# Attention and a two-layer block on one core: batch 2's products with v in float32, a first pair of quarter products interleaved, sums and a branch rearranged

## The chip, the cores and the metric

The kernel runs on one core of one Trainium2 chip. The metric is device time in microseconds of one execution, lower is better. Engines: PE = TensorE, DVE = VectorE, ACT = ScalarE, POOL = GpSimd, SP = SyncE, whose queue issues nearly all DMAs.

## The reference

Eight batches, twelve heads, 448 tokens, head size 64; then 768 to 2048 to 768 features. Inputs are float32.

```python
scores = q @ k.T / sqrt(64) - log(448)
attn = 1 / (1 + exp(-scores))
x = (attn @ v)                      # heads side by side: 3584 x 768
h = x @ w_in                        # 768 x 2048
g = h - tanh(h)
out = g @ w_out                     # 2048 x 768
```

## The kernel before

**Tiles.** Features lie on the partitions and the 448 tokens of a batch along the free axis. Two heads share 128 partitions, so a batch has six *head pairs*. `stream` counts them through batches 1 to 7 as g = 0 to 41 and takes two per turn. For a pair, `units` makes scores (`scores`, L532), ACT turns them into the weights a (`weigh`, L543, a sigmoid), and `av` (L563) multiplies them with v into a PSUM tile acc, which ACT copies to x (`evac_x`, L575 or L577).

**Precision.** A float32 operand is mostly split into two float16 parts, the rounded value and the remainder, and a product takes three float16 matmuls. The rounded part comes from ACT (`activation` with Copy and a scale), the remainder from DVE (`scalar_tensor_tensor`): for a, `split_a` (L549, L550); for x and weights, `split` (L335, L338); for w_in's sums, `parts` (L197, L199). In `stream` the class constant `AV32` says from which batch on products with v are split (`splits`): before it, a and v go to PE as float32, where one call becomes two instructions. With the split come norms of v (`norm_v`, L473 on vn), its split (`prep_v`, L518, L519) and a scale at `evac_x`. There, an x without a scale has its square taken by ACT (L592), one with a scale by POOL (L594) in four of six pairs; POOL adds the squares up (L603).

**Stages.** Batch 0 runs in `first`, whose steps follow a string, `ORDER`, one letter a step: among others, R and r convert and split weights, B is the next step of the attention stream, P two steps of the output product, Z and S splits of w_in. Batch 1 multiplies by w_in as it is (`moe1`), and meanwhile `combine` builds, for each of eight column pairs q of w_in, sums of its four quarters (L209 to L215) and their split parts. `combine` is a generator with three steps per q, driven by `made`: 14 inside `moe1`, ten at the positions `MADE` in batch 1's output product. `load` brings a q's weights in, in part after the parts before have left the same place. Batches 2 to 7 use those sums: `moe1_quarters` needs seven quarter products per column pair instead of eight (`product`, L1004, 9 matmuls of 224 columns each; the names S3, A11, S2, A22, A12, S1, S4 say which sum of w_in is taken). Results c11, c21 lie in a PSUM tile py, c12, c22 in px; ACT copies c11 to c12 (L1052) and keeps c21 and c12 (L1053, L1060), DVE adds (L1074, L1075), and the curve of g follows one or two turns later (`square`, `cube`, `curve`, `rest`, `store`).

**Output product.** `moe2` multiplies g by w_out (L1137) into po, two PSUM tiles under the tag "mm" which py also uses, and evacuates po to o (L1157 on ACT, L1159 on DVE). After each of its 96 steps `second` runs what is due by a table of positions on a scale of 56: `BLOCKS1` or `BLOCKS` (attention of the next batch), `MADE`, `TAIL` (the end of g), `FILL` and `NORMS` (loads), `PARTS` (the scale of x, then its split into quarters, by `quarter_scales`). All engines' orders, SP's too from batch 1 on, are the order in which the code issues. The end: a flag says whether a general kernel must run instead (`build_kernel`, L1518 and L1519).

```python
def second(self, b, blocks, alone, events):
    ...
    for k, _ in enumerate(self.moe2(b, self.gs)):
        now = (k + 1) * 7 / 12
        while events and events[0][0] <= now:
            events.pop(0)[1]()
```

Of the kernel before, what the change touches and what calls it, by code (L numbers as in the profile page):

```python
# [10 lines left out]
F32 = mybir.dt.float32  # L11
# [8 lines left out]
P = 128  # L20
# [15 lines left out]

class Builder:

    AV32 = 2

    EARLY = 4
    LAND = ("o", "o", 2, "v", "v", "v", 1, 0, 3, 4, 5)
# [1 line left out]
        "lurmlorumsrrsrrmmlussmvvrrssvvrlrssvvrrvruvlssrurssvvrrssvlrrsvvvursrsvs"  # L44
        "vrrssvrsrrvvvvRrRrRRRMrRRRnRrRRGMRRwtMttRtRBtwRRtMwBgttMtRtRttMBttRtRttM"
        "tMBBtRttRMtBttMttDMtRxtRtBRAtDMtttADMtBttDMttAttAttMMtAtPPtaRRBPtBbtCaBC"
        "BACPtFCCPBPCPPBZPPCSBCPPBZCBCPPCCBPCCCSZBPCCCPCXBaaAPaPPPBAPaaaBBSPPSPSZ"
        "PSZSPPPPPPSPBPPZPPPNPZPSPZSSNNPPSZPZSSPPPP"
    )

    BLOCKS = (8, 11, 16, 20, 20, 20, 27, 32, 36, 36, 36, 43, 47, 51, 52)
    TAIL = (1, 2, 3, 4, 5)
    MADE = (5, 10, 12.5, 15, 21.5, 23, 25, 29.5, 31, 34)
    FILL = (44.5, 48.5, 53.5)
    END = (0.1, 1.7, 3)
    NORMS = (4.5, 10, 13, 24, 28)
    PARTS = (1.5, 5, 8.5, 10.5)
    ALONE = 11
    BLOCKS1 = (4, 7, 8, 11, 13, 16, 20, 20, 20, 27, 32, 36, 36, 36, 43, 47, 51, 52)

# [117 lines left out]
    def combine(self):  # L178

        h = self.NC // 2  # L180
        V = self.nc.vector
        at = self.NC * self.NB * 2 * 256
        tail = self.flat[:, at : at + 4 * self.NC * P].bitcast(F32).rearrange("p (t c n) -> p t c n", t=2, c=self.NC)
        loaded = {}

        def load(q):
            if q in self.AWAY:
                loaded[q] = [self.tp.tile([P, self.NC, P], F32, name="w32", tag="t", bufs=self.TP) for _ in range(2)]
                for i, t in enumerate(loaded[q]):
# [5 lines left out]
        def parts(q, o, src, between=lambda: None):  # L195
            t = self.tp.tile([P, self.NC, 2, P], F16, name="wt", tag="t", bufs=self.TP)
            self.nc.scalar.activation(t[:, :, 0], src, AF.Copy, scale=self.Swi)  # L197
            between()
            V.scalar_tensor_tensor(t[:, :, 1], src, self.Swi, t[:, :, 0], op0=ALU.mult, op1=ALU.subtract)  # L199
            self.nc.sync.dma_start(self.w1[q, :, o : o + 2], t.rearrange("p (o c) i n -> p o c i n", c=h))  # L200

        load(0)
        for q in range(self.NF // 2):
            top, bottom = loaded.pop(q)
            a11, a12, a21, a22 = top[:, :h], top[:, h:], bottom[:, :h], bottom[:, h:]
            ahead = (q in self.AWAY) != (q + 1 in self.AWAY)
            if ahead:
                load(q + 1)
            V.tensor_tensor(a22, a21, a22, op=ALU.add)  # L209
            V.tensor_tensor(a21, a11, a21, op=ALU.subtract)  # L210
            yield 1

            def sums():
                V.tensor_tensor(a11, a22, a11, op=ALU.subtract)
                V.tensor_tensor(a12, a12, a11, op=ALU.subtract)  # L215

            parts(q, self.S3, bottom, sums)
            yield 1
            parts(q, self.S2, top)
            if not ahead:  # L220
                load(q + 1)
            yield 1
# [383 lines left out]
    def stream(self):  # L606
# [34 lines left out]

        def parts_k(g):
            if g < G:
                K[g] = self.parts(qk[g][0], sc[g][0][:, 0:1], "K", not splits(g) and g not in (2, 3))

        def parts_q(g):
            if g < G:
# [74 lines left out]
        def keep(g, cs, aa):  # L722
            if splits(g):
                aa = [self.split_a(a) for a in aa]
                if len(self.xs) < NP and g >= self.NP * (self.AV32 - 1) + 2:
                    self.x_sums()
            todo.extend((g, c, a) for c, a in zip(cs, aa))

        for g in range(0, G, 2):
# [162 lines left out]
    def quarter_scales(self, xs):  # L892

        h = self.NC // 2
        m = self.token_norms(self.ps.tile([P, 2, 512], F32, name="nm", tag="sc", bufs=2)[:, 0])
        Sx, ix = self.x_scale(m)
        self.x_sums()
        xt = self.xt
        out = self.xparts()

        def parts(c, x, ops):
            self.split(out[:, ops, c, 0], out[:, ops, c, 1], x, Sx, True)

        def pair(x):
            return x.rearrange("p (t n) -> p t n", t=2)

        yield 0
        for c in range(h):
            parts(c, pair(xs[c]), slice(self.B11, self.T1 + 1, self.T1 - self.B11))
        yield 0  # L910
        for c in range(h):
            parts(c, xt[c], slice(self.T3, self.T4 + 1))
        yield 0
        for c in range(h):
            parts(c, pair(xs[c + h]), slice(self.B21, self.B22 + 1))
        self.xready = (out, *self.h_scales(ix), m)
        yield 0

    def g_scales(self, m):
# [69 lines left out]
    def moe1_quarters(self, st, sums):  # L989
# [45 lines left out]
        def last(d):  # L1035
# [2 lines left out]
                self.load_ring(d["k"] + self.SLOTS)  # L1038
            square(d, 1)

        old, older = None, None
        for k in range(NQ):
            y = self.ps.tile([P, 512], F32, name="py", tag="mm", bufs=2)
            xt = self.ps.tile([P, 2, 512], F32, name="px", tag="sc", bufs=2)
            d = {"k": k, "x": xt, "ps": (y[:, : 2 * n], xt[:, 0, : 2 * n])}
            c11, c21, c12, c22 = y[:, :n], y[:, n : 2 * n], xt[:, 0, :n], xt[:, 0, n : 2 * n]
            kept = temp("pu", n)
            product(k, c21, self.S3, self.T3, True)
            product(k, c11, self.A11, self.B11)
            if old:  # L1050
                begin(old)
            nc.scalar.activation(c12, c11, AF.Copy)  # L1052
            nc.scalar.activation(kept[:, 0], c21, AF.Copy)  # L1053
            if older:
                rest(older)
            if old:
                cube(old, 0)
                last(old)
            product(k, c12, self.S2, self.T2)
            nc.scalar.activation(kept[:, 1], c12, AF.Copy)  # L1060
            if old:
                cube(old, 1)
                if k == 1:
                    self.Sg, self.iSg = self.g_scales(m)
            product(k, c21, self.A22, self.T4)
            product(k, c11, self.A12, self.B21)
            if older:
                store(older)
            if old:
                curve(old)  # L1070
            product(k, c12, self.S1, self.T1)
            if sums and k == 3:
                self.norm_sums(xt[:, 1])
            V.tensor_tensor(c22, c12, kept[:, 0], op=ALU.add)  # L1074
            V.tensor_tensor(c21, c21, kept[:, 1], op=ALU.add)  # L1075
            old, older = d, old

        def end():
            begin(old)
# [428 lines left out]
def build_kernel(tc, q, k, v, moe_w_in, moe_w_out, out):  # L1508
    nc = tc.nc
    args = (tc, q, k, v, moe_w_in, moe_w_out, out)  # L1510
    with ExitStack() as outer:
# [39 lines left out]
```

## Time and profile before

| | |
|---|---|
| median of 3 runs | 1152.42 us (1151.61 to 1153.48) |
| profiled execution | 1153.86 us, span 1152.1 us |
| PE busy | 1120.5 us, 97% |
| DVE busy | 809.4 us, 70% |
| ACT busy | 796.2 us, 69% |
| POOL busy | 78.2 us, 7% |
| granted clock, mean | 0.993 of 2.4 GHz |

The span is the time from the first to the last instruction; 1.8 us of the profiled execution lie outside it. Batch 0 takes the first 226 us, batch 1's first product lasts until 282 us and its output product until 381 us, and six batches of some 130 us follow. How the views are read: a wait names the instruction that came last before an engine went on; a busy PE's rows overlap, since a matmul's modelled end lies behind the start of the next.

### The profile page before, as it was taken

How to read it: one execution, taken by the hardware profiler on the slowest of the kernel's cores; microseconds unless marked ns; L12 is line 12 of the kernel's file. 1: busy time of each engine (PE TensorE's matmuls, PEld its weight loads, DVE VectorE, ACT ScalarE, POOL GpSimd, SP SyncE). 2: the span in 40 equal slices, each digit the busy share in tenths (PEclk: the TensorE clock that was granted, in tenths of full speed). 3: DMA queues.
4: the chain of work that ended last, by engine and by line, in shares of the span. 5: the costliest groups of instructions: out<-in, count | busy, mean ns of one | idle time of the engine just before them, and what ended most of it. 6: DMA issues, size and time to landing. Idle time of an engine off the chain costs nothing. (4 is left out here: it accounts for less than half of the span.)

```text
span 1152.1 us, 20209 instructions
## 1 busy us (share of the span) xinstructions
PE 1120.5 (97%) x8096; PEld 677.8 (59%) x8096; DVE 809.4 (70%) x1403; ACT 796.2 (69%) x1289; POOL 78.2 (7%) x58
## 2 busy tenths in 40 slices
PE   9999998999989999999999999999999999999997
PEld 3355433454434894449844696448944597449953
DVE  6987598778787766886667866787768766665710
ACT  7965685646968667885688767886688866754600
POOL 0000000000120000300022000210012000310000
PEclk9999999999998999999999999999999999999999
DMA  9992271176444652227423453246421561026200
GB/s 367 391 349 73 62 212 30 58 221 191 147 138 144 215 188 86 81 65 253 146 80 98 160 193 112 73 160 217 170 94 60 188 239 54 17 91 227 100 24 27
DMA packets 78694, 167.13 MB, mean 145 GB/s; under 512 B 24320, under 2 KB 58240, under 8 KB 71808
## 3 DMA queue, kind: packets, MB, share of 16 engines
q1 hardware_dynamic: 78304, 165.42, 42.7%
q8 instruction: 65, 1.06, 0.4%
q10 hardware_dynamic: 288, 0.34, 0.1%
q14 instruction: 37, 0.30, 0.1%
HBM read 137.43 MB, written 28.31 MB: 144 GB/s over the span
## 5 line engine op out<-in xcount | busy, mean ns | idle before, releaser
L1137 PE MATMUL po<-g,wo 128*128 128x448 f16 x2304 | 453.1, 353 | 4.2 <-ACT o L1157 4.2
L1137 PEld LDWEIGHTS <-wo 128*128 128x128 f16 x2304 | 219.4, 98 | 226.4 <-issue 31.8
L1004 PEld LDWEIGHTS <-wi 128*128 128x128 f16 x3024 | 289.9, 98 | 14.1 <-issue 10.9
L550 DVE SCALAR_TENSOR_TENSOR ahl<-a,ahl 128x896 f16<-128x896 f32 x126 | 162.3, 1323 | 105.8 <-ACT ahl L549 104.6
L543 ACT ACTIVATE a<-sc,nls,rn 128x896 f32<-128x896 f32 x147 | 155.8, 1090 | 51.1 <-PE sc L532 51.0
L1004 PE MATMUL py<-wi 128*128 128x224 f16 x1728 | 181.3, 259 | 0.0
L1004 PE MATMUL px<-wi 128*128 128x224 f16 x1296 | 141.4, 259 | 9.9 <-ACT px L1052 9.9
L549 ACT ACTIVATE ahl<-a 128x896 f16<-128x896 f32 x126 | 113.2, 942 | 0.6
L948 DVE SCALAR_TENSOR_TENSOR g<-m,Sg,g 128x896 f16<-128x896 f32 x64 | 73.6, 1150 | 41.3 <-ACT g L947 41.1
L532 PE MATMUL sc<-Q,K 64*128 64x448 f16 x1008 | 102.4, 356 | 0.0
L1014 ACT ACTIVATE u<-py,ih 128x448 f32<-128x448 f32 x48 | 30.5, 635 | 77.7 <-DVE py L1075 76.2
L563 PE MATMUL acc<-ahl,vhl 128*64 128x448 f16 (+1 forms) x864 | 82.5, 360 | 1.6 <-ACT tn L484 0.9
L594 POOL TENSOR_TENSOR x<-x 128x448 f32<-128x448 f32 x24 | 27.9, 1161 | 752.2 <-ACT x L577 640.2
L947 ACT ACTIVATE g<-m,Sg 128x896 f16<-128x896 f32 x64 | 66.2, 1034 | 14.9 <-DVE m L1028 10.7
L532 PEld LDWEIGHTS <-K 64*128 64x128 f16 x1008 | 35.9, 97 | 64.9 <-issue 41.3
L1245 PE MATMUL ph<-x,wi 128*128 128x448 f32 x192 | 73.8, 540 | 0.0
L563 PEld LDWEIGHTS <-vhl 128*64 128x64 f16 (+1 forms) x864 | 40.0, 110 | 42.8 <-issue 22.1
L1017 DVE SCALAR_TENSOR_TENSOR m<-px,ihk,u 128x448 f32<-128x448 f32 x48 | 32.8, 683 | 37.9 <-ACT u L1014 37.9
L1245 PEld LDWEIGHTS ph<-x,wi 128*128 128x128 f32 x192 | 36.2, 190 | 33.2 <-issue 32.4
L954 PE MATMUL ph<-xhl,wi 128*128 128x448 f16 x288 | 55.0, 352 | 0.7 <-DVE m L1102 0.7
L1028 DVE SCALAR_TENSOR_TENSOR m<-q,m 128x896 f32<-128x896 f32 x48 | 52.0, 1084 | 0.7
L1025 ACT ACTIVATE q<-u,b 128x896 f32<-128x896 f32 x48 | 49.5, 1031 | 0.2
(184 smaller groups left out, 1198.2 us busy)
## 6 DMA issues: line engine op xcount, KB each, us to landing
wi<-w SPq DMA_DIRECT2D x53, 1344.0 KB, 6.0
out<-o SPq DMA_DIRECT2D x47, 224.0 KB, 2.0
knn<-k SPq DMA_DIRECT2D x45, 224.0 KB, 2.6
qnn<-q SPq DMA_DIRECT2D x44, 224.0 KB, 2.6
rawo<-moe_w_out SPq DMA_DIRECT2D x22, 384.0 KB, 5.5
raw<-moe_w_in SPq DMA_DIRECT2D x13, 512.0 KB, 8.2
vn<-v SPq DMA_DIRECT2D x24, 256.0 KB, 2.9
w<-wi SPq DMA_DIRECT2D x16, 384.0 KB, 6.2
```

What stands on the lines that cost most here:

```text
L532: self.nc.tensor.matmul(ps[i * m : (i + 1) * m, h, : self.S], K[i][r, w, c * P : c * P + m], Q[i][r, x, :], start=(n == 0), stop=(n == len ...
L543: self.nc.scalar.activation(a[:, 0], ps[:, :, : self.S], AF.Sigmoid, bias=self.nls, scale=scale)
L549: nc.scalar.activation(A[:, 0], a[:, 0], AF.Copy, scale=A_SCALE)
L550: nc.vector.scalar_tensor_tensor(A[:, 1], a[:, 0], A_SCALE, A[:, 0], op0=ALU.mult, op1=ALU.subtract)
L563: self.nc.tensor.matmul(acc[i][h * D : (h + 1) * D, : self.S], v[k, w, 2 * QT + h if half else h * QT + c], A[k, x, h], start=(n == 0 and ...
L947: nc.scalar.activation(g[:, 0], m, AF.Copy, scale=Sg)
L948: nc.vector.scalar_tensor_tensor(g[:, 1], m, Sg, g[:, 0], op0=ALU.mult, op1=ALU.subtract)
L954: self.nc.tensor.matmul(ph, self.wi[:, self.slot(c, k), part, e * P : (e + 1) * P], xhl[c][:, x, :], start=(i == 0), stop=(i == len(prods) ...
L1004: nc.tensor.matmul(out, w[:, a, c, i], x[:, b, c, j], start=start and k == 0, stop=k == len(prods) - 1, skip_group_check=True,)
L1028: V.scalar_tensor_tensor(d["m"], d.pop("q"), C0, d["m"], op0=ALU.add, op1=ALU.mult)
L1137: nc.tensor.matmul(po[:, :S], self.wo[:, e * self.NF + rows[f // 2][f % 2], w, at : at + P], moving(gs[f // 2][:, x], f % 2), start=(f == ...
L1245: nc.tensor.matmul(ph[:, e, :S], self.fp32(self.wi, self.slot(c, k))[:, 0, e * P : (e + 1) * P], xs[c], start=(c == 0), stop=(c == self.NC ...
```

## The change

It does six things. `AV32` goes from 2 to 3: batch 2's products with v are float32 ones, its v is neither normed nor split, its a not split; by the condition in `add_squares`, all squares of its x are then ACT's. In `ORDER` the letters B and Z stand the other way round relative to P ("SZBPCCC" becomes "SZPBCCC"): an attention step comes after a step of the output product. `combine` makes all four sums of a q before its first yield. `TAIL` and `MADE` get other positions. `quarter_scales` leaves the split of the lower quarters of x (B21, B22) to a function `xrest`, called in the next `moe1_quarters`, and `PARTS` has one position less. `moe1_quarters` runs S3 and A11 of column pairs 0 and 1 and their copies before S2 of pair 0; from pair 2 on the order is as it was. The `If` has its other block as the one to fall into.

```diff
-    AV32 = 2
+    AV32 = 3
...
-        "BACPtFCCPBPCPPBZPPCSBCPPBZCBCPPCCBPCCCSZBPCCCPCXBaaAPaPPPBAPaaaBBSPPSPSZ"
+        "BACPtFCCPBPCPPBZPPCSBCPPBZCBCPPCCBPCCCSZPBCCCPCXBaaAPaPPPBAPaaaBBSPPSPSZ"
...
-    TAIL = (1, 2, 3, 4, 5)
-    MADE = (5, 10, 12.5, 15, 21.5, 23, 25, 29.5, 31, 34)
+    TAIL = (1, 2, 4.5, 5)
+    MADE = (6, 9, 12.5, 15, 18, 22, 25, 29, 31, 34)
...
-    PARTS = (1.5, 5, 8.5, 10.5)
+    PARTS = (1.5, 5, 8.5)
...
             V.tensor_tensor(a22, a21, a22, op=ALU.add)
             V.tensor_tensor(a21, a11, a21, op=ALU.subtract)
+            V.tensor_tensor(a11, a22, a11, op=ALU.subtract)
+            V.tensor_tensor(a12, a12, a11, op=ALU.subtract)
             yield 1
-
-            def sums():
-                V.tensor_tensor(a11, a22, a11, op=ALU.subtract)
-                V.tensor_tensor(a12, a12, a11, op=ALU.subtract)
-
-            parts(q, self.S3, bottom, sums)
+            parts(q, self.S3, bottom)
...
-        yield 0
-        for c in range(h):
-            parts(c, pair(xs[c + h]), slice(self.B21, self.B22 + 1))
         self.xready = (out, *self.h_scales(ix), m)
+
+        def rest():
+            for c in range(h):
+                parts(c, pair(xs[c + h]), slice(self.B21, self.B22 + 1))
+
+        self.xrest = rest
...
+        def first(k):
...
+            product(k, d["c"][2], self.S3, self.T3, True)
+            product(k, d["c"][0], self.A11, self.B11)
+            return d
+
+        def copies(d):
+            nc.scalar.activation(d["c"][1], d["c"][0], AF.Copy)
+            nc.scalar.activation(d["kept"][:, 0], d["c"][2], AF.Copy)
+
+        def second(d):
+            product(d["k"], d["c"][1], self.S2, self.T2)
+            nc.scalar.activation(d["kept"][:, 1], d["c"][1], AF.Copy)
+
+        d = first(0)
+        copies(d)
+        self.xrest()
+        new = first(1)
+        copies(new)
+        second(d)
...
+            if k == 0:
+                d = new
+                begin(old)
+                second(d)
+                cube(old, 0)
+                last(old)
+                cube(old, 1)
+                self.Sg, self.iSg = self.g_scales(m)
+            elif k + 1 < NQ:
+                d = first(k + 1)
...
-        with tc.If(small == 0, preferred_fallthrough_block=False):
+        with tc.If(small == 0, preferred_fallthrough_block=True):
```

Three places show how instructions move. The changed file's lines up to `quarter_scales` stand 4 lower in number (L543 is L539 there), those of `moe2` 19 higher (L1157 is L1176).

ACT late in batch 0, where `ORDER` is changed; a are sigmoids, x and its square follow, sqn on vn are norms of v, o evacuates the output product, wi is a split of w_in. Before:

```order
L335 ACTIVATE wi<-wi,swi_s 128x2x256
L543 ACTIVATE a_1552<-sc,nls,rn 128x896
L543 ACTIVATE a_1554<-sc,nls,rn 128x896
L575 ACTIVATE x_1562<-acc 128x448
L592 ACTIVATE x_1564<-x_1562 128x448
L473 ACTIVATE sqn,ss_123<-vn 128x512
L473 ACTIVATE sqn,ss_123<-vn 128x384
L1157 ACTIVATE o<-po,iK 128x448
```

And now:

```order
L331 ACTIVATE wi<-wi,swi_s 128x2x256
L1176 ACTIVATE o<-po,iK 128x448
L539 ACTIVATE a_1557<-sc,nls,rn 128x896
L539 ACTIVATE a_1559<-sc,nls,rn 128x896
L571 ACTIVATE x_1567<-acc 128x448
L588 ACTIVATE x_1569<-x_1567 128x448
L539 ACTIVATE a_1621<-sc,nls,rn 128x896
L539 ACTIVATE a_1623<-sc,nls,rn 128x896
```

The evacuation o stands directly behind the split wi, ahead of the sigmoids; the two norms of v are gone.

ACT at the start of batch 2's quarter products; ahl are copies of a, wi<-x the split of the lower quarters of x, px<-py and pu<-py the copies of the first quarter products. Before:

```order
L549 ACTIVATE ahl<-a_3611 128x896
L549 ACTIVATE ahl<-a_3616 128x896
L335 ACTIVATE wi<-x_3125,Sx 128x2x224
L335 ACTIVATE wi<-x_3314,Sx 128x2x224
L335 ACTIVATE wi<-x_3443,Sx 128x2x224
L1157 ACTIVATE o<-po,iK 128x448
L1052 ACTIVATE px<-py 128x224
L1053 ACTIVATE pu<-py 128x224
L1060 ACTIVATE pu<-px 128x224
L1014 ACTIVATE u<-py,ih 128x448
```

And now:

```order
L545 ACTIVATE ahl<-a_3423 128x896
L545 ACTIVATE ahl<-a_3428 128x896
L1176 ACTIVATE o<-po,iK 128x448
L1050 ACTIVATE px<-py 128x224
L1051 ACTIVATE pu<-py 128x224
L331 ACTIVATE wi<-x_2986,Sx 128x2x224
L331 ACTIVATE wi<-x_3143,Sx 128x2x224
L331 ACTIVATE wi<-x_3251,Sx 128x2x224
L1050 ACTIVATE px<-py 128x224
L1051 ACTIVATE pu<-py 128x224
L1055 ACTIVATE pu<-px 128x224
```

The three splits of x have moved behind the first two copies, and the copies of the second column pair come before the first S2's copy (pu<-px).

DVE in batch 1's output product, near the last q of `combine`; wt are remainders of w_in's sums, ahl those of a, the four rows of 128x224 are `x_sums`, the rows of 128x384 the sums of w_in's quarters. Before:

```order
L199 SCALAR_TENSOR_TENSOR wt<-wi,swi_s,wt 128x6x128 x2
L550 SCALAR_TENSOR_TENSOR ahl<-a_3103,ahl 128x896
L550 SCALAR_TENSOR_TENSOR ahl<-a_3105,ahl 128x896
L886 TENSOR_TENSOR wo<-x_3125,x_2703 128x224
L887 TENSOR_TENSOR x_2703<-x_2703 128x224
L888 TENSOR_TENSOR wo<-x_3125,x_2703 128x224
L889 TENSOR_TENSOR wo<-x_3125,wo 128x224
L1159 TENSOR_SCALAR o<-po,iK 128x448
L209 TENSOR_TENSOR wi<-wi 128x384
L210 TENSOR_TENSOR wi<-wi 128x384
```

And now:

```order
L198 SCALAR_TENSOR_TENSOR wt<-wi,swi_s,wt 128x6x128 x2
L882 TENSOR_TENSOR wo<-x_2986,x_2651 128x224
L883 TENSOR_TENSOR x_2651<-x_2651 128x224
L884 TENSOR_TENSOR wo<-x_2986,x_2651 128x224
L885 TENSOR_TENSOR wo<-x_2986,wo 128x224
L1178 TENSOR_SCALAR o<-po,iK 128x448
L208 TENSOR_TENSOR wi<-wi 128x384
L209 TENSOR_TENSOR wi<-wi 128x384
L210 TENSOR_TENSOR wi<-wi 128x384
L211 TENSOR_TENSOR wi<-wi 128x384
```

The remainders of a are gone, and all else stands in the same order.

## Rows read from the trace of the kernel before

**Rows 1.** The page, part 1: busy us (share of span) and instructions.
```profile
PE 1120.5 (97%) x8096; PEld 677.8 (59%) x8096; DVE 809.4 (70%) x1403; ACT 796.2 (69%) x1289; POOL 78.2 (7%) x58
```

**Rows 2.** Waits of PE, whole span: waited for, us in total, times, longest.
```profile
PE px L1004 <- ACT px L1052: 9.9, 6, 1.9
PE pbn L482 <- ACT sqn L473: 5.9, 2, 5.3
PE po L1137 <- ACT o L1157: 4.2, 1, 4.2
...
PE acc L563 <- ACT tn L484: 0.9, 1, 0.9
PE ph L954 <- DVE m L1102: 0.7, 2, 0.6
PE acc L563 <- DVE ahl L550: 0.4, 1, 0.4
```

**Rows 3.** Windows: PE, PEld, DVE, ACT, POOL busy (x instructions), PEclk, DMA share, GB/s.
```profile
177.60:182.00 4.40, 4.35 (x25) 1.40 (x24) 1.58 (x9) 0.54 (x2) 0.00 (x0) 0.61 0.14 52
345.50:352.40 6.90, 6.69 (x43) 2.93 (x42) 5.84 (x14) 5.32 (x8) 0.00 (x0) 0.54 0.16 58
```

**Rows 4.** Timeline of batch 0: start, us, engine, line, operation, tiles, [idle before <-releaser].
```profile
177.65 2.32 PE L1137 MATMUL po<-g,wo 128*128 128x448 f16 x6 [4.21 <-ACT o L1157]
...
180.33 0.56 DVE L426 TENSOR_REDUCE mo<-wl 128x1 f32<-128x384 f32 x1 [2.61 <-PE wl L301]
...
190.13 1.08 ACT L543 ACTIVATE a<-sc,nls,rn 128x896 f32<-128x896 f32 x1
...
192.41 0.74 PE L532 MATMUL sc<-Q,K 64*128 64x448 f16 x6
```

**Rows 5.** Timeline, PE: products with v in float32 (batch 1), in float16 (later).
```profile
189.09 3.39 PE L563 MATMUL acc<-a,vn 128*64 128x448 f32 x20
...
206.91 2.48 PE L563 MATMUL acc<-a,vn 128*64 128x448 f32 x12
...
361.29 1.89 PE L563 MATMUL acc<-ahl,vhl 128*64 128x448 f16 x18
...
375.41 2.58 PE L563 MATMUL acc<-ahl,vhl 128*64 128x448 f16 x30
```

**Rows 6.** Timeline of batch 1's output product, DVE and ACT.
```profile
335.13 3.10 DVE L550 SCALAR_TENSOR_TENSOR ahl<-a,ahl 128x896 f16<-128x896 f32 x2 [2.32 <-ACT ahl L549]
...
341.49 0.56 DVE L214 TENSOR_TENSOR wi<-wi 128x384 f32<-128x384 f32 x1
```

**Rows 7.** Timeline, first quarter product of batch 2; then L1004 in ns (min/median/max).
```profile
380.87 1.77 ACT L549 ACTIVATE ahl<-a 128x896 f16<-128x896 f32 x2
...
381.35 1.89 PE L1004 MATMUL py<-wi 128*128 128x224 f16 x18
...
384.22 0.61 ACT L1157 ACTIVATE o<-po,iK 128x448 f32<-128x448 f32 x1
...
385.13 1.02 PE L1004 MATMUL px<-wi 128*128 128x224 f16 x9 [1.89 <-ACT px L1052]
...
385.44 1.87 DVE L338 SCALAR_TENSOR_TENSOR wi<-x,Sx,wi 128x448 f16<-128x448 f32 x3
...
L1004 PE MATMUL py<-wi x1728: 259/259/259, 381.3 to 1087.7; 128*128 128x224 f16 x192
```

**Rows 8.** SP's queue at the branch and after it: ns min/median/max, first, last start.
```profile
L1519 SPq EVENT_SEMAPHORE  x8: 17/17/17, 1145.7 to 1147.8; - x8
...
L1519 SPq COMPARE_BRANCH  x2: 38/46/53, 1145.6 to 1147.9; - x2
...
L1547 SPq EVENT_SEMAPHORE  x10: 17/28/28, 1150.8 to 1152.0; - x10
```

More of the change, by code (lines that the diff above doesn't have):

```diff
@@ L193, in load, with parts @@
                 self.nc.sync.dma_start(tail, self.w32[q])
-        def parts(q, o, src, between=lambda: None):
+        def parts(q, o, src):
             t = self.tp.tile([P, self.NC, 2, P], F16, name="wt", tag="t", bufs=self.TP)
             self.nc.scalar.activation(t[:, :, 0], src, AF.Copy, scale=self.Swi)
-            between()
             V.scalar_tensor_tensor(t[:, :, 1], src, self.Swi, t[:, :, 0], op0=ALU.mult, op1=ALU.subtract)
@@ L643, in parts_k @@
             if g < G:
-                K[g] = self.parts(qk[g][0], sc[g][0][:, 0:1], "K", not splits(g) and g not in (2, 3))
+                K[g] = self.parts(qk[g][0], sc[g][0][:, 0:1], "K", g < NP and g not in (2, 3))
         def parts_q(g):
@@ L724, in keep @@
                 aa = [self.split_a(a) for a in aa]
-                if len(self.xs) < NP and g >= self.NP * (self.AV32 - 1) + 2:
-                    self.x_sums()
+            if len(self.xs) < NP and g >= NP + 2:
+                self.x_sums()
             todo.extend((g, c, a) for c, a in zip(cs, aa))
@@ L1039, in last @@
             square(d, 1)
+        def first(k):
+            y = self.ps.tile([P, 512], F32, name="py", tag="mm", bufs=2)
+            xt = self.ps.tile([P, 2, 512], F32, name="px", tag="sc", bufs=2)
+            d = {"k": k, "x": xt, "ps": (y[:, : 2 * n], xt[:, 0, : 2 * n]), "kept": temp("pu", n)}
+            d["c"] = y[:, :n], xt[:, 0, :n], y[:, n : 2 * n], xt[:, 0, n : 2 * n]
+            product(k, d["c"][2], self.S3, self.T3, True)
[13 more added lines that the diff above has]
+        second(d)
         old, older = None, None
         for k in range(NQ):
[L1043 to L1050, printed above, removed]
+            c11, c12, c21, c22 = d["c"]
+            if k > 1:
                 begin(old)
-            nc.scalar.activation(c12, c11, AF.Copy)
-            nc.scalar.activation(kept[:, 0], c21, AF.Copy)
-            if older:
+                copies(d)
                 rest(older)
-            if old:
                 cube(old, 0)
                 last(old)
-            product(k, c12, self.S2, self.T2)
-            nc.scalar.activation(kept[:, 1], c12, AF.Copy)
-            if old:
+                second(d)
                 cube(old, 1)
-                if k == 1:
-                    self.Sg, self.iSg = self.g_scales(m)
             product(k, c21, self.A22, self.T4)
@@ L1072, in moe1_quarters @@
             if sums and k == 3:
-                self.norm_sums(xt[:, 1])
-            V.tensor_tensor(c22, c12, kept[:, 0], op=ALU.add)
-            V.tensor_tensor(c21, c21, kept[:, 1], op=ALU.add)
+                self.norm_sums(d["x"][:, 1])
+            V.tensor_tensor(c22, c12, d["kept"][:, 0], op=ALU.add)
+            V.tensor_tensor(c21, c21, d["kept"][:, 1], op=ALU.add)
             old, older = d, old
+            if k == 0:
+                d = new
+                begin(old)
+                second(d)
+                cube(old, 0)
[4 more added lines that the diff above has]
+                d = first(k + 1)
         def end():
```

## The prediction

> **What bounds the kernel now.** I read the page's busy shares first, then TensorE's list of waits, then the stretches where it waits. PE is busy for 97% of the span [rows 1]: work taken off other engines is worth only the wait that it ends, and work put on PE is paid in full unless PE stands there anyway. The list of waits [rows 2] holds nearly all idle time of PE, and the change touches each of its rows except the start-up: six waits of a quarter product for a copy by ScalarE, 9.9 us, the longest 1.9; one for the evacuation of an output tile, 4.2; two for the squares of K and Q, 5.9, of which one is 5.35; then 0.9, 0.7 and 0.4. A wait costs a little more than its row says, since idle time is counted from the modelled end of the matmul ahead. Eighteen matmuls last 1.89 us, one lasts 0.259 [rows 7], so their pitch is 1.63 / 17 = 0.096 us and the next could start 0.16 us before the row ends. I add 0.16 per wait. After the two longest waits the clock was granted at 0.61 of 2.4 GHz for 4.4 us and at 0.54 for 6.9 us [rows 3], so part of each stretch ran at 1.2 GHz. What that took is 4.4 x 0.39 = 1.7 us and 6.9 x 0.46 = 3.2 us. Before both, PE had stood idle for over 4 us.
>
> **The change part by part**, against the profiled execution's 1153.86 us (span 1152.1).
>
> *1. An output's evacuation ahead of the attention step in batch 0 (the two letters in ORDER).* PE waits 4.21 us for o of L1157, which ScalarE runs after two sigmoids, an x, its square and two norms of v [rows 4]. In the new order o stands right behind a split of w_in, and the products of the tile before come ahead of the scores. The wait and the slow clock behind it cost 4.21 + 0.16 + 1.7 = 6.1 us. Not all comes back. VectorE stood idle for 2.61 us until PE's sums of w_out came (L426) and works almost without a pause after it; it can move forward by 2.6 us only. PE hangs on that chain at its scores of 192.41: these need the buffer that the sigmoid of 190.13 frees at 190.13 + 1.08 = 191.21 [rows 4], 1.2 us early. So PE gains 2.6 + 1.2 = 3.8 us. Bounds: 2.6 if the slack is gone too, 6.1 if the removed work on v shortens the chain enough.
>
> *2. Batch 2's products with v in float32: PE's price.* Both forms are in the trace [rows 5]: 20 float32 instructions 3.39 us where 30 float16 take 2.58, and 12 in 2.48 where 18 take 1.89, at full clock. That is 0.81 + 0.59 = 1.40 us per pair of head pairs, three pairs: 4.2 us more, all on PE, in batch 1's output product. The four more squares on ScalarE (L592, where POOL did them) take less than the copies that ScalarE loses in the same stretch, below.
>
> *3. What the same part removes.* ScalarE loses 21 copies of a (L549; two take 1.77 us [rows 7]) and the norms of v, VectorE 21 remainders (L550) and the split of v. In that stretch stand the waits 5.35, 0.53, 0.95 and 0.39, in sum 7.2; with 4 x 0.16 and the slow clock's 3.2 they cost 11.0 us. The long one hangs together like this [rows 6]: two L550 keep VectorE for 3.10 us from 335.13; its sums of w_in's quarters come after them, ScalarE's L197 starts at 341.49 after 4.44 us of waiting for these sums, and the sigmoids and squares that PE needs stand behind L197. Without the L550 the chain ahead is 3 us shorter, and the sigmoids of the step before stand behind two L197 that are no longer late, which I put at another 2 to 3 us. That is enough for 5.35. The 0.95 and 0.39 are waits for work that goes (L550 itself, and a copy that queued behind L549). Of the 0.53 most stays, since scores come just before. I take 10.6 back. Late next is the load of the last w_in quarters ahead of those sums; an idle VectorE would wait there. Lower end 8, if half of the long wait stays; that it stays whole is a rival below.
>
> *4. Sums in one step.* The same four sums, earlier, so nothing is added. Two waits of 0.7 us in batch 1's first product (for L1102, in rows 2) cost 1.0 with their ends: the first stands behind a chain that part 1 moves forward as well, the second behind sums that now come earlier. Against it, in two other places L1102 now stands behind two more sums. I take 0.9, with ends 0 and 1.0.
>
> *5. First pair interleaved.* Six times PE waits for L1052, which copies PSUM behind three splits of x and one o on ScalarE: 9.9 + 6 x 0.16 = 10.8 us. In the new order S3 and A11 of two quarters run first, 36 matmuls in 3.45 us. From rows 7: copies of a end at 380.87 + 1.77 = 382.64, o of 0.61 follows until 383.26, so c11's copy ends at about 383.6, well before S2 at 385. The second quarter needs the PSUM buffer that o frees and could start at 383.08: with the handover 0.26 us lost, five times, 1.3 us (the last batch has no attention). The moved splits of x are wanted by A12, from about 386.8; VectorE does them from 385.44 at 0.62 each, so the third is ready at 387.3, when PE reaches it at 387.4: just in time. So 9.5 us. Lower end 6, if A12 waits 0.7 in each of five batches; upper end 10.8. The splits leave the stage before, where PE does not wait for them.
>
> *6. Branch turned.* In the old layout each engine falls into the short block, where SP waits for the last outputs until 1147.8, and jumps over the general kernel afterwards: SP's jump is at 1147.9, its next instruction at 1150.8, 2.9 us [rows 8]. Now the first branch jumps, at 1145.6, and lands at 1148.5, with the outputs landed meanwhile; the eight short waits of the block end near 1148.75, and the end block is adjacent: 2.05 us. Ends: 0 if the second jump pays again, 2.9. The Trainium skill ("Runtime: NRT & Kernel Launch", Instruction fetch mechanics) says that a taken branch out of the window of two pages must wait for its target's page; both layouts have one such jump, so by it alone nothing would change in number, and the sum would be 20.6 instead of 22.65. No row here shows two such jumps side by side.
>
> Sum: 3.8 - 4.2 + 10.6 + 0.9 + 9.5 + 2.05 = 22.65 us, hence 1153.86 - 22.65 = 1131.2 for an execution like the profiled one. The median of the runs shown is 1.44 us lower; from it, **1129.8 us**. With all good ends 27.6 come off (1124.8), with the bad ones 2.6 - 4.2 + 8 + 0 + 6 + 0 = 12.4 (1140).
>
> **Rivals.** *The long wait stays.* L197 still stands ahead of the sigmoids, and its sums still need a load. If that load, or the sums' place behind the quarter sums of x, keeps L197 late, 5.35 + 0.16 + 3.2 = 8.7 us stay: 1138.5. For it: the order of these rows is unchanged. Against: VectorE, not the load, ended that wait, and it gets 3 us earlier.
>
> *The jump costs as much as before.* One far jump in each layout: if the engines or the end block wait for a page either way, 2.05 us are missing: 1131.9. For it: the number of far jumps. Against: the old one starts only after the outputs have landed. The skill's rule on branches, above, is the one behind this rival.
>
> *The first pair's wait moves.* The second quarter waits for o and A12 for the split of x, together as long as L1052 was waited for: 1139.3. Against: each hand-over, taken from rows 7, is late by 0.3 us at most.
>
> *Slower.* The splits of x come so late that PE stands at A12 as it stood at 345, followed by the slow clock: 5.35 + 0.16 + 3.2 = 8.7 us in each of five batches, 43.5 us; the rest brings 13 us without part 5, so about 1183. It would have to wait behind VectorE's split of v, whose load SP issues late. It decides from a loss of 22.65 / 5 = 4.5 us per batch, that is a third split ready at 391.9 instead of 387.3. Against: the same three instructions with the same work ahead end at 387.3 today. That the change doesn't do what it says can be ruled out by the order rows ahead of this.
>
> **How the numbers follow.** Forecast 0.66; long wait stays 0.13; jump as before 0.13; first pair's wait moves 0.05; slower 0.03. The range goes from the good ends to the first and third rivals, 1125 to 1139. About 0.2%, 2.3 us, is what a measurement of this kernel tells from no change. All cases but the last are faster by far more; 0.02 is for parts that cancel.
>
> **What would show it.** Right: PE's list of waits without L1052, without the 4.2 and the 5.35; clock at 1.0 in all stretches from 200 us on; 96 float32 rows more for L563 and a sixth of its 864 float16 rows fewer; batch 1's output product 6 us shorter; short waits, 0.3 us, before the second py; SP's end block 2 us earlier relative to the last output. Wrong: a wait of PE for sqn of 5 us, a wait at A12 for L338's successor over 0.5 us, PE waiting for a or pbn around 184 to 190 for more than 2.5 us in all, or the end block 2.9 us behind SP's second branch.

## The result, and the profile after

The changed kernel takes 1131.07 us (median of 4 runs, 1130.45 to 1133.24) where the kernel before took 1152.54 beside it: a ratio of 0.9817, interval 0.9800 to 0.9834, or 21.5 us less. Forecast were 1129.8 and a range of 1125 to 1139. A second set of runs gave 1130.95 (ratio 0.9818, 0.9805 to 0.9831).

The page's first part, which answers to [rows 1]:

```profile
PE 1118.3 (99%) x8043; PEld 674.0 (60%) x8048; DVE 777.7 (69%) x1367; ACT 777.1 (69%) x1260; POOL 70.6 (6%) x54
```

PE was idle for 31.6 us of its span and is now for 10.9 (span less busy time). Its list of waits, whole span without the start-up's (waited for: us in total, times, longest), answers to [rows 2]:

```profile
PE sc L528 <- ACT a L539: 1.2, 1, 1.2
...
PE py L1003 <- DMA wi<-w: 0.4, 1, 0.4
```

The waits for L1052, for o, for the squares, for tn, m and ahl are gone. Two new waits stand there: 1.2 us for a sigmoid in batch 0, 0.4 for a load into the ring of w_in's sums. The granted clock is now 1.00 at both places of [rows 3], late in batch 0 and behind the squares of batch 1's output product, which PE reaches at 333.6 us here (windows: busy us of PE, PEld, DVE, ACT, POOL, then PEclk, DMA share, GB/s):

```profile
168.00:190.00 22.00, 20.57 (x134) 8.48 (x131) 20.09 (x41) 16.07 (x29) 1.75 (x2) 1.00 0.24 77
333.70:340.00 6.30, 6.30 (x46) 2.27 (x45) 5.27 (x15) 4.13 (x7) 0.02 (x1) 1.00 0.49 154
```

The spans of the two profiled executions, 1152.1 and 1129.2 us, cut at the starts of PE's rows (first product with v; first ph<-xhl; end of the last of these; first quarter product of batch 2; end of the last po):

| stretch | before | after | less | terms of the forecast |
|---|---|---|---|---|
| start, to the first product with v | 12.26 | 10.94 | 1.3 | none |
| batch 0 | 214.47 | 210.29 | 4.2 | part 1: 3.8 |
| batch 1, first product | 55.71 | 54.64 | 1.1 | part 4: 0.9 |
| batch 1, output product | 98.91 | 91.89 | 7.0 | parts 2 and 3: 6.4 |
| batches 2 to 7 | 762.76 | 754.70 | 8.1 | part 5: 9.5 |
| end, behind PE | 7.99 | 6.74 | 1.25 | part 6: 2.05 |

The start is no part of the change: it takes 10.83 to 12.33 us in the profiles of all the kernels here, which share it. In the stretch of parts 2 and 3 the chain of [rows 6] moved forward against PE. Before, VectorE's sums of w_in's quarters started 4.25 us behind the start of a row of PE's output product:

```profile
336.07 4.15 PE L1137 MATMUL po<-g,wo 128*128 128x448 f16 x21
...
340.32 0.55 DVE L209 TENSOR_TENSOR wi<-wi 128x384 f32<-128x384 f32 x1
```

In the changed kernel they start 2.28 us ahead of the same row, so 6.5 us earlier against it:

```profile
327.37 0.55 DVE L208 TENSOR_TENSOR wi<-wi 128x384 f32<-128x384 f32 x1
...
329.65 4.15 PE L1156 MATMUL po<-g,wo 128*128 128x448 f16 x21
```

Three more places, in the trace of the changed kernel. First batch 0, which answers to [rows 4] (timeline: start, us, engine, line, operation, idle before and what ended it):

```profile
171.61 0.62 ACT L1176 ACTIVATE o<-po,iK 128x448 f32<-128x448 f32 x1
...
172.28 1.29 PE L1156 MATMUL po<-g,wo 128*128 128x448 f16 x6
...
184.93 0.94 ACT L331 ACTIVATE wo<-wo,swo_s 128x768 f16<-128x768 f32 x1 [2.70 <-DVE un L484]
...
185.77 1.08 ACT L539 ACTIVATE a<-sc,nls,rn 128x896 f32<-128x896 f32 x1
...
186.90 0.74 PE L528 MATMUL sc<-Q,K 64*128 64x448 f16 x6 [1.23 <-ACT a L539]
```

The evacuation o ends at 172.23, and PE goes on at 172.28 with no wait for it. Then the scores of [rows 4]'s last line wait: the sigmoid whose buffer they need (185.77) stands behind a split of w_out that had waited 2.70 us for VectorE. The next, the first quarter products of batch 2, answers to [rows 7]:

```profile
367.09 0.15 DVE L849 TENSOR_TENSOR ih<-ix,swi_i 128x1 f32<-128x1 f32 x1
367.28 0.15 DVE L850 TENSOR_SCALAR ihk<-ih 128x1 f32<-128x1 f32 x1
...
367.76 3.76 PE L1003 MATMUL py<-wi 128*128 128x224 f16 x36
...
368.97 0.62 ACT L1176 ACTIVATE o<-po,iK 128x448 f32<-128x448 f32 x1
...
369.69 0.34 ACT L1050 ACTIVATE px<-py 128x224 f32<-128x224 f32 x1
...
372.13 1.87 DVE L334 SCALAR_TENSOR_TENSOR wi<-x,Sx,wi 128x448 f16<-128x448 f32 x3
...
372.22 2.19 PE L1003 MATMUL py<-wi 128*128 128x224 f16 x18
```

The 36 matmuls run without a stop for the copy, but take 3.76 us where they take 3.61 in batch 7, which has no attention of a next batch beside it; the 18 behind the first px take 2.19 instead of 1.89. So 0.15 us are lost before the second pair's buffer is free, and 0.30 before A12 has its third split of x, which ends at 374.00 (372.13 + 1.87). Last, SP at the end, at the branch (L1538) and behind it (L1566), which answers to [rows 8] (ns min/median/max, first and last start):

```profile
L1538 SPq EVENT_SEMAPHORE  x8: 17/17/17, 1127.3 to 1127.9; - x8
L1538 SPq COMPARE_BRANCH  x1: 50/50/50, 1123.9 to 1123.9; - x1
```

```profile
L1566 SPq EVENT_SEMAPHORE  x10: 17/28/28, 1128.0 to 1129.2; - x10
```

SP jumps at 1123.9 and is back at 1127.3; the end block follows its eight waits directly.

### The profile page after: what moved, and what is told of

It is laid out like the page before. It is cut to its first block, busy times and chain, and to the rows that moved or that the text cites. A ratio compares the mean times of both kernels' runs of the same rounds, so it can differ in the third digit from the quotient of the medians.

```text
span 1129.2 us, 20011 instructions
## 1 busy us (share of the span) xinstructions
PE 1118.3 (99%) x8043; PEld 674.0 (60%) x8048; DVE 777.7 (69%) x1367; ACT 777.1 (69%) x1260; POOL 70.6 (6%) x54
## 4 chain that ended last, share of the span: by engine, by line
PE 86%; DVE 9%; ACT 2%; issue 2%; DMA 1%; DVEq 0%; SPq 0%; ACTq 0%
PE po L1156 33%; PE py L1003 12%; PE px L1003 10%; PE sc L528 8%; PE acc L559 8%; PE ph L1264 6%; PE ph L953 5%; DVE wi L334 3%; DVE ahl L546 2%; DVE stb L277 1%; DMA wi<-w 1%; PE cs L303 1%; PE warm L115 1%; ACT sqn L469 1%; DVE Q L506 0%
## 5 line engine op out<-in xcount | busy, mean ns | idle before, releaser
L546 DVE SCALAR_TENSOR_TENSOR ahl<-a,ahl 128x896 f16<-128x896 f32 x105 | 135.1, 1321 | 95.4 <-ACT ahl L545 94.3
L539 ACT ACTIVATE a<-sc,nls,rn 128x896 f32<-128x896 f32 x147 | 155.9, 1091 | 56.9 <-PE sc L528 56.8
L545 ACT ACTIVATE ahl<-a 128x896 f16<-128x896 f32 x105 | 94.5, 943 | 0.5
L559 PE MATMUL acc<-ahl,vhl 128*64 128x448 f16 (+1 forms) x720 | 67.2, 356 | 0.0
L590 POOL TENSOR_TENSOR x<-x 128x448 f32<-128x448 f32 x20 | 22.9, 1143 | 598.1 <-ACT x L573 598.1
L559 PE MATMUL acc<-a,vn 128*64 128x448 f32 (+1 forms) x288 | 54.4, 553 | 0.1
L599 POOL TENSOR_TENSOR x<-x,x 128x448 f32<-128x448 f32 x21 | 35.0, 1665 | 304.7 <-ACT x L588 303.5
```

Of the source, the lines that this page charges most:

```text
L539: self.nc.scalar.activation(a[:, 0], ps[:, :, : self.S], AF.Sigmoid, bias=self.nls, scale=scale)
L545: nc.scalar.activation(A[:, 0], a[:, 0], AF.Copy, scale=A_SCALE)
L546: nc.vector.scalar_tensor_tensor(A[:, 1], a[:, 0], A_SCALE, A[:, 0], op0=ALU.mult, op1=ALU.subtract)
L559: self.nc.tensor.matmul(acc[i][h * D : (h + 1) * D, : self.S], v[k, w, 2 * QT + h if half else h * QT + c], A[k, x, h], start=(n == 0 and ...
```

## The experiments

Stretches of every profile, cut as above (us; the last column is the median of the runs; before is 1152.26 to 1152.54 beside them):

| kernel | batch 0 | batch 1, first | batch 1, output | batches 2 to 7 | end | median |
|---|---|---|---|---|---|---|
| before | 214.47 | 55.71 | 98.91 | 762.76 | 7.99 | 1152.54 |
| changed | 210.29 | 54.64 | 91.89 | 754.70 | 6.74 | 1131.07 |
| changed, again | 210.41 | 54.64 | 91.89 | 754.06 | 6.74 | 1130.95 |
| old first pair | 210.82 | 54.64 | 91.89 | 762.77 | 6.75 | 1140.54 |
| AV32 = 2 | 210.06 | 56.76 | 98.11 | 756.07 | 6.79 | 1141.08 |
| old ORDER | 212.70 | 54.64 | 91.89 | 754.72 | 6.99 | 1132.97 |
| old branch | 210.48 | 54.63 | 91.90 | 754.11 | 9.15 | 1133.65 |
| before, AV32 = 3 | 212.73 | 54.64 | 92.41 | 762.76 | 8.92 | 1144.28 |
| old sums | 210.57 | 54.64 | 92.40 | 754.10 | 6.75 | 1131.71 |
| no branch | 210.31 | 54.64 | 91.89 | 754.08 | 4.22 | 1129.25 |
| AV32 = 4 | 210.77 | 54.65 | 92.69 | 759.54 | 7.16 | 1136.37 |
| S1 ahead of A12 | 210.71 | 54.64 | 91.89 | 752.58 | 6.60 | 1129.34 |
| both mended | 209.00 | 54.64 | 91.89 | 752.58 | 6.56 | 1128.42 |

A stretch repeats to 0.1 us, with three exceptions: batch 0 (210.1 to 210.8 in the nine profiles with the new ORDER, as a wait of 0 to 0.7 us for tn comes and goes), batches 2 to 7 (a ring load) and the end (the landing of the last output).

**The first pair, undone.** Edit, from the changed kernel: `moe1_quarters`, `quarter_scales` and

```diff
-    PARTS = (1.5, 5, 8.5)
+    PARTS = (1.5, 5, 8.5, 10.5)
```

> The changed kernel with the old order of the first column pairs (S2 of pair 0 directly behind S3 and A11, the split of the lower quarters of x back in the output product, PARTS with four positions). Theory A, the parts add up: 8.0 us slower than the changed kernel, since the six stretches of quarter products were 1.61 (four times), 1.01 and 0.59 us shorter in it; PE's list shows six waits of px for the copy on ScalarE again, five of about 1.9 us. Rival: batch 2's float32 products had already taken copies of a off ScalarE ahead of the first of these stretches, so that the first wait is under 1 us: then only 7 us slower.

Batches 2 to 7 take 762.77 us, 8.1 to 8.7 more than in the changed kernel, and all else stays. Its list of waits:

```profile
PE px L1000 <- ACT px L1048: 9.9, 6, 1.9
```

All six waits are back at their old size, the first included: the rival falls. The old order takes 762.8 us in these batches with the other parts of the change (here) and without them (before). The median is 9.5 us higher, where 8.0 was expected; beyond the 8.1 to 8.7 of these batches, batch 0 is up to 0.5 longer in this profile, which is within its spread.

**AV32 back to 2.**

```diff
-    AV32 = 3
+    AV32 = 2
```

> The changed kernel with AV32 at 2, batch 2's products with v in float16 parts again. Theory A, the work on a and v made the long wait: PE's wait of about 5 us for the squares of K and Q in batch 1's output product comes back with the slow clock, PE is 4.2 us less busy, together 4 to 7 us slower. Rival B, the sums in one step and their new positions ended that wait by themselves: no wait over 1 us, and the kernel is about 4 us faster than the changed one (the price of the float32 products saved).

PE's waits of this kernel that the changed one has not, or has smaller, whole span:

```profile
PE pbn L478 <- ACT sqn L469: 3.0, 1, 3.0
PE acc L559 <- DVE ahl L546: 2.2, 2, 1.7
PE acc L559 <- ACT tn L480: 1.7, 3, 0.8
PE ph L953 <- DVE m L1121: 1.7, 1, 1.7
PE py L1003 <- DMA wi<-w: 1.6, 2, 0.8
```

2.1 us more in batch 1's first product and 6.2 in its output product; with 1.4 in batches 2 to 7, where the ring's load is waited for, the median is 10.0 higher, more than the 4 to 7 expected. B falls. Theory A has the cause right and the sizes not: with the new sums the wait for the squares is 2.96 us, not about 5, but smaller waits around it are longer. VectorE and ScalarE at that place:

```profile
332.16 1.17 DVE L546 SCALAR_TENSOR_TENSOR ahl<-a,ahl 128x896 f16<-128x896 f32 x1 [0.77 <-ACT ahl L545]
...
336.01 0.56 DVE L209 TENSOR_TENSOR wi<-wi 128x384 f32<-128x384 f32 x1
...
336.60 0.94 ACT L197 ACTIVATE wt<-wi,swi_s 128x768 f16<-128x768 f32 x1 [3.35 <-DVE wi L209]
...
339.41 0.57 ACT L469 ACTIVATE sqn<-knn 128x448 bf16<-128x448 f32 x1
```

L197 waits for the sums (L209) again; from the remainder of a (332.16) to the sums VectorE works without a pause. Two sigmoids and the squares stand behind L197, as [rows 6] had it.

This run also has the two norms of v in batch 0 again, now behind o:

```profile
171.77 0.61 ACT L1176 ACTIVATE o<-po,iK 128x448 f32<-128x448 f32 x1
...
175.36 0.61 ACT L469 ACTIVATE sqn<-vn 128x512 bf16<-128x512 f32 x1
```

Batch 0 takes 210.06 us all the same, no longer than in the changed kernel: with o ahead of them, the norms cost it nothing.

**AV32 at 3 alone, from the kernel before.** (The two further edits keep the parts of K and the `x_sums` where they were; the changed kernel has them too.)

```diff
-    AV32 = 2
+    AV32 = 3
...
-                K[g] = self.parts(qk[g][0], sc[g][0][:, 0:1], "K", not splits(g) and g not in (2, 3))
+                K[g] = self.parts(qk[g][0], sc[g][0][:, 0:1], "K", g < NP and g not in (2, 3))
...
-                if len(self.xs) < NP and g >= self.NP * (self.AV32 - 1) + 2:
-                    self.x_sums()
+            if len(self.xs) < NP and g >= NP + 2:
+                self.x_sums()
```

> The kernel before with AV32 at 3 alone. Theory A, the work on a and v in float16 made the waits of batch 1's output product: the wait of 5.35 us and the slow clock go though the sums stand where they stood, the wait for o in batch 0 shrinks by 1.5 us to about 2.7 (no norms of v ahead of it), PE is 4.2 us busier: 1143 to 1146. Rival B, the sums' old places keep a late wait: over 2 us of waits stay between 285 and 380 us, and the time is above 1147.

PE's waits of this kernel, whole span, without the start-up's:

```profile
PE px L1004 <- ACT px L1052: 9.9, 6, 1.9
PE po L1137 <- ACT o L1157: 2.5, 1, 2.5
...
PE pbn L482 <- ACT sqn L473: 0.4, 1, 0.4
```

Theory A holds, and the median, 1144.28, lies in its range. This edit alone brings batch 1's first product to 54.64, where the two waits for m go, its output product to 92.41, and batch 0 down by 1.74: the wait for o is 2.5 us without the norms of v.

**ORDER, undone.** The two strings differ in one B and one P that change places; the Z ahead of them stays where it was.

```diff
-        "BACPtFCCPBPCPPBZPPCSBCPPBZCBCPPCCBPCCCSZPBCCCPCXBaaAPaPPPBAPaaaBBSPPSPSZ"
+        "BACPtFCCPBPCPPBZPPCSBCPPBZCBCPPCCBPCCCSZBPCCCPCXBaaAPaPPPBAPaaaBBSPPSPSZ"
```

> The changed kernel with the old ORDER, an attention step ahead of the output product's step in batch 0. Theory A, the order of o on ScalarE is what made that wait: it comes back, less the 1.5 us of the two norms of v, which float32 products in batch 2 no longer need: 2.7 us, and the wait of 1.2 us at the scores goes: 1.5 us slower, 3 with a slow clock. Rival, the norms of v made the wait and the swap is worth nothing: within 0.5 us of the changed kernel or faster by 1.2.

The wait in PE's list that this kernel has besides those of the changed one:

```profile
PE po L1156 <- ACT o L1176: 2.4, 1, 2.4
```

Batch 0 takes 2.41 us more (1.9 to 2.6 against the spread above), and the median is 1.9 higher, between the two figures of theory A: the wait of 2.4 us is followed by a stretch at a clock of 0.61. The rival falls. The worth of the swap depends on what else is there. Against the kernel before, the swap with the norms of v still in place (the run with AV32 = 2) brings batch 0 down by 4.4 us, the missing norms without the swap (before, AV32 = 3) by 1.7, and both together by 4.2. Both shorten the same wait for o, and with the swap PE stops next at the sigmoid either way (1.23 us with the norms and without), so their gains do not add up.

**The sums, undone** (`combine` with two sums after its first yield, and):

```diff
-    TAIL = (1, 2, 4.5, 5)
-    MADE = (6, 9, 12.5, 15, 18, 22, 25, 29, 31, 34)
+    TAIL = (1, 2, 3, 4, 5)
+    MADE = (5, 10, 12.5, 15, 21.5, 23, 25, 29.5, 31, 34)
```

> The changed kernel with combine, MADE and TAIL as before. Theory A: this part is worth little by itself, 0 to 1 us slower than the changed kernel, two short waits of 0.7 us at the most in batch 1's first product. Rival B, it is the part that lets AV32 at 3 end the long wait: a wait of over 2 us in batch 1's output product, 3 to 6 us slower.

PE's list has a wait of 0.7 us for tn in batch 0, which is within that batch's spread, and one that is new in this kernel:

```profile
PE pbn L482 <- ACT sqn L473: 0.4, 1, 0.4
```

0.5 us more in batch 1's output product: this wait of 0.35 us for the squares, with its 0.16. Batch 1's first product does not change, so the waits for m there were not this part's.

**The branch, undone, and taken out.**

```diff
-        with tc.If(small == 0, preferred_fallthrough_block=True):
+        with tc.If(small == 0, preferred_fallthrough_block=False):
```

> The changed kernel with the old layout of the branch. Theory A: the end block comes 2.9 us behind SP's second branch again, and the time from the issue of the last output to the end of the span grows from 5.7 to about 6.9 us: 1.2 us slower. Rival, far jumps cost the same wherever they are: within 0.3 us. Third: the old layout lands the last output in 2.7 us, not 3.7, since no code is fetched at the same time; if the landing stays at 3.7 here, that was not the cause.

SP at the branch, and behind it:

```profile
L1538 SPq EVENT_SEMAPHORE  x8: 17/17/17, 1125.0 to 1128.0; - x8
L1538 SPq COMPARE_BRANCH  x2: 38/46/53, 1124.9 to 1128.1; - x2
```

```profile
L1566 SPq EVENT_SEMAPHORE  x10: 17/28/28, 1131.3 to 1132.6; - x10
```

SP waits for the landing until 1128.0, jumps at 1128.1 and is in the end block at 1131.3, 3.2 us later. From the issue of the last output (1124.49) to the end of the span are 8.1 us, where the changed kernel has 5.7; the median is 2.6 higher. Theory A is right in kind, and its 1.2 us half the size: in the old layout the time behind the issue was 6.9 us with a landing after 2.6 us (before), 7.9 with 3.0 (before, AV32 = 3) and 8.1 with 3.5 here. The rival falls. The third guess falls too: in the old layout the output can land after 3.5 us as well, so the layout by itself does not set the landing.

```diff
-        with tc.If(small == 0, preferred_fallthrough_block=True):
-            with ExitStack() as ctx:
-                General(ctx, *args).run()
```

> The changed kernel without the branch and without the general kernel behind it, which does not run on this data: what the jump costs. Theory A, the engines' one far jump and the landing of the last output run side by side, 3.4 and 3.7 us: without the jump the end waits for the landing alone; if landing stays at 3.7 us the span's end behind the last issue stays at 5.7 us, no gain over 0.5 us. Rival: fetching code delays the landing; then it lands in about 2.7 us and 1 us is gained.

The DMA view of the last 9 us, first of the kernel without the branch, then of the changed one (queue: packets, MB, share; issues: KB, median us to landing):

```profile
q14 instruction: 1, 0.01, 0.4%
...
out<-o SPq DMA_DIRECT2D x1, 112.0 KB, 2.3
```

```profile
q14 instruction: 7, 0.06, 2.9%
q8 instruction: 2, 0.03, 1.7%
...
out<-o SPq DMA_DIRECT2D x1, 112.0 KB, 3.7
```

The end is 4.22 us long, 2.5 less, the median 1.8 lower, and the last output lands after 2.3 us. Theory A falls. Its rival comes nearer, but it had 1 us for the gain: the loads on the instruction queues (1 against 9 packets) go with a later landing, 2.6 to 3.9 us in the twelve profiles that have a branch. That these loads are what delays it is not shown. How much of the 2.5 us is landing and how much the jump itself was not taken apart.

**The price of float32 alone.**

```diff
-    AV32 = 3
+    AV32 = 4
```

> The changed kernel with AV32 at 4: batch 3's products with v in float32 too, in a stretch where PE waits for nothing. It measures the price of the float32 products by itself. Theory: 96 of them take 4.2 us more than 144 float16 ones, all of it PE's: the stretch from the first quarter product of batch 2 to that of batch 3 grows from 131.3 to 135.5 us less what its first pair gains from a ScalarE without copies of a (0.3 at batch 3's start), the kernel is 4 us slower than the changed one. Rival: float32 products leave PE's weight loads shorter time behind, the price is half, 2 us.

PE in batch 2's output product of this kernel (timeline), now with float32 products; the first one of batch 4, at the end, is in float16:

```profile
444.50 3.39 PE L559 MATMUL acc<-a,vn 128*64 128x448 f32 x20
...
497.25 2.58 PE L559 MATMUL acc<-ahl,vhl 128*64 128x448 f16 x30
```

The output product of batch 2 lasts 84.19 us (419.00 to 503.19) where the changed kernel takes 80.83 (418.21 to 499.04), that of batch 1 92.69 where it takes 91.89: 3.36 + 0.80 = 4.16 us. The theory's price holds, and the rival's half falls. The first stretch of quarter products shrinks from 47.88 to 47.44 us: its rows of 36 and of 18 matmuls take 3.61 and 1.89 us here, as ScalarE has no copies of a ahead of o, and VectorE, which stood idle for 5.95 us ahead of the splits of x, has the third ready 5.00 us behind the start of the stretch. The median is 5.3 us higher; more than the price went to another wait, which PE's list has for the ring:

```profile
PE py L1003 <- DMA wi<-w: 2.2, 2, 1.2
```

**What was left, mended.** In `moe1_quarters`, and FILL:

```diff
-    FILL = (44.5, 48.5, 53.5)
+    FILL = (44.5, 48.5, 50.5)
...
+            if k == 0:
+                product(k, c12, self.S1, self.T1)
             product(k, c11, self.A12, self.B21)
...
-            product(k, c12, self.S1, self.T1)
+            if k:
+                product(k, c12, self.S1, self.T1)
```

> The changed kernel with S1 of column pair 0 ahead of its A12, so that the split of x has 0.86 us more, and the third load into the ring at 50.5 instead of 53.5. Theory A: the row of 18 matmuls of 2.19 us behind the first px goes back to 1.89 in batches 2 to 6 (0.30 each, 1.5 us), and the 0.4 us wait for the ring's load in batch 3 (0.6 us of that batch) goes: 2.1 us faster than the changed kernel, 1129. Rival: the later A12 makes the curve and the copies behind it late, and the third pair waits for that instead: no gain.

PE in batch 4 (timeline), S2, A22 and then S1 in single rows of 9, where A22 and A12 stood as one row of 18:

```profile
634.40 1.03 PE L1003 MATMUL px<-wi 128*128 128x224 f16 x9
635.26 1.03 PE L1003 MATMUL py<-wi 128*128 128x224 f16 x9
636.12 1.03 PE L1003 MATMUL px<-wi 128*128 128x224 f16 x9
```

Each of batches 2 to 6 is 0.30 us shorter than in the undisturbed profiles of the changed kernel, 1.5 in all (754.06 to 752.58); the median fell by 1.7. Nothing else became late: the rival falls. No ring wait stands here, but the changed kernel had none in its second profile either; whether FILL did anything is open.

```diff
-        "...APaPPPBAPaaaBBSPPSPSZ"
+        "...APaPPPBPaaaBABSPPSPSZ"
```

> S1 ahead of A12 in pair 0 and the earlier ring load as in the run above, and in ORDER one step of the split of w_out (an A) behind an attention step instead of ahead of it, so that the sigmoid which PE's scores of 186.9 us wait for no longer stands behind a ScalarE copy that waits 2.7 us for VectorE. Theory A: PE's wait of 1.23 us goes, 1.2 to 1.4 us less in batch 0: 2.9 to 3.1 us faster than the changed kernel, 1128.1. Rival: the scores wait for VectorE's parts of Q or K instead, or the sums of squares behind them: only the 1.7 us of the run above.

PE's list of waits of this kernel, all of it but the start-up's:

```profile
PE acc L559 <- ACT tn L480: 0.2, 1, 0.2
```

Batch 0 takes 209.00 us, 1.3 to 1.4 less, with no wait for a sigmoid. This kernel, the mends together, is the fastest: 1128.42 us (5 runs, 1127.36 to 1128.65), ratio to before 0.9792 (0.9779 to 0.9805). Beside it the changed kernel gave 1130.95, so 2.5 us less where 2.9 to 3.1 were expected; the two stretches fell by 2.8 to 2.9 together, and the medians differ by a little less. Of batch 0's part, up to 0.7 us is its spread; that the wait of 1.2 us is gone is in the list.

> The changed kernel once more, beside the two others on one chip. If the wait of 0.42 us for the ring's load in batch 3 belongs to the kernel, batch 3 takes 132.2 us again, if it comes and goes, 131.6; the same for the end behind the last output's issue, 5.7 us in its first profile.

Batch 3 takes 131.62 us here, where the first profile had 132.22: the ring's wait comes and goes. The end is 5.7 us behind the last issue again, though this time the output landed after 3.0 us instead of 3.7. In the nine profiles with this layout it is 5.5 to 6.1 us, with landings after 2.8 to 3.9 us, and 3.2 us without the branch. So in these profiles the jump sets the end of the changed layout, and the landing hardly does.

## Why the prediction was right, and where its steps were not

**Total.** The six terms gave 22.65; the two profiled executions differ by 22.9 in span, of which 1.3 is the start. Without it 21.6 remain, so the terms were some 1.1 us too good, and that is nearly the distance of 1129.8 from the measured 1131.07. That the total is so near is in part luck: parts 1 to 4 gave 1.2 us more than forecast, parts 5 and 6 gave 2.2 less.

**Part 1, the swap: right, and 0.4 us low.** Batch 0 gained 4.2 for 3.8 foreseen, and 4.4 from the swap with the norms of v in place, so the step could leave these norms out of its sum. The scores named as the next limit are indeed where PE waits now. Their sigmoid came 3.0 us earlier, counted from the first product with v (177.87 before, 174.83 now), where the step let this chain move by 2.6.

**Parts 2 and 3, right to 0.1 us.** Price forecast 4.2, measured 4.16. Gain forecast 10.6; AV32 alone brought 6.50 net in that stretch, 10.7 with the price. That AV32 is the cause is shown both ways, by it alone and by its return to 2. That it acts through VectorE's remainders and L197 is read from the rows; no run takes the remainders away and leaves the rest. The step put 3 us and another 2 to 3 for this chain, and the sums start 6.5 us earlier against PE. "Late next is the load" was wrong and cost nothing: in the changed kernel VectorE stands idle for 4.15 us ahead of `x_sums` and these sums, but for x from ScalarE (L571). The rival "long wait stays" did not come.

**Part 4, right in size by accident.** The 1.1 us in batch 1's first product are AV32's (the run before with AV32 = 3), not the sums'; these bring 0.5 us, and elsewhere. The step counted on part 1 to move the chain of the first m forward as well. With AV32 at 2 the swap moved m by 3.3 us and PE by 4.4 (from the first product with v), and the wait for m grew from 0.6 to 1.7 us. With AV32 at 3, the first m ends 1.8 us sooner behind the start of the stretch than before (12.5 us in the run with AV32 at 3 alone, for 14.3), and PE does not wait; which piece of AV32's work makes the 1.8 us was not taken apart.

**Part 5, mis-sized: 8.1 for 9.5.** The 0.26 us at the second py was 0.15. "Just in time" at A12 failed by 0.30 us: the prediction had the third split ready 5.95 us behind the start of the stretch and PE there at 6.05; the third came at 6.24, and PE, which waited 0.30 for it, wanted it at 5.94. VectorE began them 0.28 us later than before (4.37 us behind the start, not 4.09). Two rows of 0.15 us (367.09 and 367.28, the scales of h) had moved ahead of them with the rest of the generator and were not counted. With S1 first the 0.30 goes, and it goes too where VectorE has no work on a and v ahead (AV32 = 4). Together 0.45 in each of five batches, where 0.26 was allowed; a ring load took another 0.6 in this profile, and without it the part brings 8.7.

**Part 6, right in kind.** 2.05 was forecast, 1.25 to 2.4 measured, according to how late the output lands in the old layout. The jump took 3.4 us, not 2.9. The Trainium skill ("Runtime: NRT & Kernel Launch", Instruction fetch mechanics) holds that a branch to code outside the window waits for that code to be fetched. The trace agrees so far: SP stands still for 3.2 us behind its jump in the old layout and for 3.4 in the new one, and the instruction queues load 9 packets in the last 9 us, against 1 without the branch. The rival drawn from that rule, equal numbers of jumps and so equal time, falls: the number is equal, but one jump follows the landing and the other runs beside it.

## What to carry to other kernels

Work added to the engine that sets the time can pay when it takes work off a chain that this engine waits for: 4.2 us of PE bought 10.7. To see it, follow each wait back through the queues of the engines ahead, to the instruction that is late there, and ask what stands ahead of *that*. Two parts that shorten the same wait share its worth: the swap alone gave 4.4 us, the missing norms alone 1.7, both 4.2, so one run that undoes a part does not tell what that part brings by itself. When one piece of work is moved out of a generator, count the small instructions that change place with it; a step that is "just in time" on paper needs a second order ready, here a product that can go first.

## What the runs showed of the hardware

The slow clock came behind shorter waits too, and what it took did not shrink with them. After 2.45 us of waiting (before, AV32 = 3) and after 2.96 us (AV32 = 2) the granted clock was (windows: PE, PEld, DVE, ACT, POOL busy, PEclk, DMA share, GB/s):

```profile
175.20:179.60 4.40, 4.40 (x26) 1.41 (x26) 3.95 (x12) 1.10 (x1) 0.62 (x1) 0.61 0.14 52
```

```profile
303.00:306.00 3.00, 2.98 (x17) 1.49 (x16) 2.55 (x3) 2.56 (x4) 1.71 (x2) 1.00 0.24 90
340.60:347.50 6.90, 6.68 (x43) 2.89 (x42) 5.83 (x13) 5.32 (x8) 0.00 (x0) 0.54 0.16 57
```

These are 0.61 and 0.54 of 2.4 GHz, so the clock was partly at 1.2 GHz, as much as after 4.21 and 5.35 us at the same two places [rows 3]. Behind a wait of 1.71 us (303 to 306) it stayed at 1.00, and so it did behind those of 1.89. So a wait shortened from 5.35 to 2.96 us gave back nothing of its clock, while in the changed kernel, where both waits are gone, both places have 1.00; by the estimate from [rows 3] that is 1.7 and 3.2 us beyond the waits.

The last output landed after 2.3 us without a branch and after 2.6 to 3.9 us with one. The instruction queues load more packets with the branch (9 against 1); whether that is the cause stays open.
